# Turning one batch's q and k by the DMA crossbar and rearranging the loads around the turns, in an attention + MLP kernel

## The chip, the cores and the metric

One core of one Trainium2 chip. The metric is device time of one execution in microseconds (us), lower is better. Most executions of one kernel agree within 1.5%. TensorE is called PE, VectorE DVE, ScalarE ACT, GpSimd POOL, SyncE SP. SP computes nothing here: it only issues DMAs, one after the other. The granted clock of a view is the share of its full clock rate at which PE was allowed to run.

## The reference, cut to what matters

```python
def _attn_ref(q, k, v, lam):                 # q, k, v: (4, 8, 768, 64) float32
    for b in range(nb):                      # blocks of 64 positions
        intra = einsum('bhic,bhjc->bhij', qb, kb) * Dmask[None]
        intra = einsum('bhij,bhjd->bhid', intra, vb)
        inter = einsum('bhid,bhde->bhie', qb * lam_pow[None], kv_state)
        out[:, :, sl] = intra + inter
        kv_state = lam_block * kv_state + einsum('bhsd,bhse->bhde', kb * rev_pow, vb)

def reference(...):
    x = attention output as (3072 tokens, 512)
    h = x @ w_in                             # 512 -> 2048
    g = h * (1.0 / (1.0 + exp(-1.702 * h)))
    return g @ w_out                         # 2048 -> 512
```

## The kernel before

The kernel goes through six waves of 512 tokens. For each wave it computes attention, then MLP1 (w_in), then MLP2 (w_out). Attention of wave w+1 runs between the MLP matmuls of wave w. Waves 0 and 1 have two half waves, each of 256 positions of one batch ("batch 0" and "batch 1" of wave 1 below: `c` = 0 and 1). Waves 2 to 5 take 128 positions of all four batches.

Scores need q and k with the head dimension on the partitions, so both must be transposed ("turned"). PE can do it (`turn_pe`, 8 matmuls against an identity, then a copy out of PSUM), or the DMA crossbar (`turn_dma`):

```python
    def turn_dma(w, c, nm):
        y = work.tile([P, 2 * NP, P], bf16, tag=f"{nm}T{c}", name=f"{nm}T")
        nc.sync.dma_start_transpose(out=y, in_=cast[w, c, nm].rearrange("p b c -> p (b c)"))
        trans[w, c, nm] = y
```

Before, waves 0 and 1 are turned by PE, waves 2 to 5 by the crossbar. `do_cast` is the DVE instruction that makes `ks` and `qs` (bf16) out of the loaded k and q; a turn waits for it. Loads, crossbar turns and output stores all go through SP, in program order. The order of everything beside the MLP is set by positions among the MLP items:

```python
        for w in range(NW):
            n = len(main)
            main += mlp_items(w)
            e = len(main)
            x = w + 1
            if x < ND:                                  # ND = 2: attention of wave 1
                for c in range(HF):
                    t, d = n + 24 + 5 * c, n + 19 + 7.5 * c
                    side += [(d, (do_cast, x, c, "k", nc.vector)), ...
                             (t, (turn_pe, x, c, "k", (act_copy, dve_copy)[c])),
                             (t + 1 + c, (turn_pe, x, c, "q", (act_copy, dve_copy)[c])),
                             (t + 3, (start, x, c)), (t + 6 - c, (end, x, c))]
            elif x < NW:
                for c in range(HF):
                    tk, tq = (n + 2.1 + 2 * c, n + 4 + c) if x == ND else (n + 4 + 2 * c, n + 5 + 2 * c)
                    side += [(tk, (do_cast, x, c, "k", nc.vector)), (tk, (turn_dma, x, c, "k")),
                             (tq, (do_cast, x, c, "q", nc.vector)), (tq, (turn_dma, x, c, "q")), ...]
                if x == ND:
                    side += [(n + 7, (stores,))]        # wave 0's eight output stores, kept back till here
                t = n + 16
                side += [(t, (n_two, x, 0)), (t + 4, (n_two, x, 1)), (t + 9, (n_rest, x))]
            if w + 2 < NW:
                side += [(n + (12 if w else 20), (load, w + 2))]
```

`n_two` are the scores of a wave. PE runs them in order: the first four matmuls need the turned k and q of the first two batches (c = 0), the next four those of the other two (c = 1), and so on in turn. So the last q turn holds up all but the first four of a group of 16.

Of the kernel before, what the change touches and what calls it, by code (L numbers as in the profile page):

```python
# [24 lines left out]
def kernel(  # L25
# [13 lines left out]
    nc = tc.nc  # L39
    f32 = mybir.dt.float32  # L40
    bf16 = mybir.dt.bfloat16
    B, H, S, D = q.shape
# [3 lines left out]
    ND = 2  # L46
# [14 lines left out]
    NW = S // P  # L61
# [9 lines left out]
    HF = 2  # L71
# [64 lines left out]
    def fill(n, new=False):  # L136
        if new:
            fill_ps[0] = ps.tile([P, W], f32, tag="mm", bufs=3, name="ps_fill")
        for _ in range(n):
            nc.tensor.matmul(fill_ps[0], zero[:, 0:P], zero, start=True, stop=True)  # L140
# [47 lines left out]
    cast, trans, masked, xT, g_of, h_ps, o_ps, t_ps = {}, {}, {}, {}, {}, {}, {}, {}  # L188

    def acc(name, dt=f32, shape=None, tag="a"):  # L190
        return ps.tile(shape or [P, 4, P], dt, tag=tag, bufs={"a": 5, "mm": 3}[tag], name=name)
# [35 lines left out]
    def turn_pe(w, c, nm, copy=act_copy, g=None):  # L227
        x = cast[w, c, nm]
        rr = list(range(NP)) if g is None else [2 * g, 2 * g + 1]
        t = acc("ps_t", bf16, [P, len(rr), 2, P])  # L230
        for i, r in enumerate(rr):
            for a in range(2):
                nc.tensor.transpose(t[:, i, a, :], x[:, a, r * P : (r + 1) * P], ident)
        if g in (None, 0):
            trans[w, c, nm] = work.tile([P, 2 * NP, P], bf16, tag=f"{nm}T{c}", name=f"{nm}T")
        copy(trans[w, c, nm][:, 2 * rr[0] : 2 * rr[0] + 2 * len(rr)], t.rearrange("p r a s -> p (r a) s"))

    def turn_dma(w, c, nm):
        y = work.tile([P, 2 * NP, P], bf16, tag=f"{nm}T{c}", name=f"{nm}T")
        nc.sync.dma_start_transpose(out=y, in_=cast[w, c, nm].rearrange("p b c -> p (b c)"))  # L240
        trans[w, c, nm] = y

    def q_of(w, c, rows, r, blk):
        return trans[w, c, "q"][rows, 2 * r : 2 * r + 2, D * blk : D * blk + D]

    def d_scores(w, c, pp):
        kT = trans[w, c, "k"]
        s2 = [acc("ps_s") for _ in range(2)]
        for i in range(2):
            r = 2 * pp + i  # L250
            for a in range(2):
                for blk, bs in enumerate((A, Z)):
                    for h, hs in enumerate((A, Z)):
                        nc.tensor.matmul(s2[h][bs, 2 * i + a, :], kT[hs, 2 * r + a, bs], q_of(w, c, hs, r, blk),  # L254
                                         start=True, stop=True)
        for h in range(2):
            sm = work.tile([P, 2, 2, P], bf16, tag="sm", bufs=8, name="sm")
            nc.vector.tensor_tensor(sm.rearrange("p i a s -> p i (a s)"), s2[h].rearrange("p (i a) s -> p i (a s)", i=2),  # L258
                                    mask_d.rearrange("p o a b s -> p o (a b s)").to_broadcast([P, 2, 2 * P]), op=MUL)
            masked[w, c, pp, h] = sm  # L260
# [145 lines left out]

    def mlp_items(w):
        if w < ND:
            f = 4 if w == 0 else 8
            items = [(mlp1_half, w, c, fc) for c in range(HF) for fc in range(0, f, 2) if w or c or fc]  # L410
            items += [(mlp1, w, fc) for fc in range(f, FFC)]
        else:
            items = [(mlp1, w, fc) for fc in range(FFC)]
        if w == 0:
            items += [(mlp2, w, g, j) for j in range(NCH) for g in range(3)]
            return items + [(mlp2, w, 3, j) for j in range(NCH)]
        items += [(mlp2, w, g, j) for g in range(G) for j in range(NCH)]
        if w == NW - 1:
            items = items[:-NCH]
            for c0, c1 in ((0, 256), (256, 384), (384, 512)):  # L420
                items += [(mlp2, w, G - 1, j, c0, c1) for j in range(NCH)]
        return items

    def gate_pool(x):
        nc.gpsimd.tensor_copy(behind_q, x)
# [4 lines left out]
    with tc.manual_schedule():  # L430
        u32 = mybir.dt.uint32
        for x in kv_sb:
            nc.vector.memset(x.rearrange("p b r s -> p (b r s)").bitcast(u32), 0)
        nc.scalar.activation(warm, q_pow[:, 0, 0:1], GELU)
        fill(5)
        for g in range(2):
            do_cast(0, 0, "k", nc.vector, g)
            turn_pe(0, 0, "k", act_copy, g)
            fill(2)
        for g in range(2):  # L440
            do_cast(0, 0, "q", nc.vector, g)
            turn_pe(0, 0, "q", act_copy, g)
            fill(2 - 2 * g)
        gate_pool(loaded[0, 0, "v"][0:1, 0, 0:1])
        load_w_in(0)
        cast_v(0, 0, (act_copy, act_copy))
        d_scores(0, 0, 0)
        fill(1)
        d_scores(0, 0, 1)
        fill(3)  # L450
        for g in range(2):
            do_cast(0, 1, "k", nc.gpsimd, g)
        for j in (1, 2):
            load_w_in(j)
        one = d_state(0, 0, False, "mm")
        two = d_state(0, 0, True, "mm")
        fill(1)
        d_keep(*one)
        d_keep(*two)
        oa, oz = d_out(0, 0, "mm")  # L460
        d_x(0, 0, 0, oa, act_copy)
        d_x(0, 0, 1, oz, act_copy)
        do_cast(0, 1, "q", nc.vector, 0)
        do_cast(0, 1, "q", nc.vector, 1)
        turn_pe(0, 1, "k", dve_copy)
        turn_pe(0, 1, "q", act_copy, 0)
        fill(2, True)
        turn_pe(0, 1, "q", act_copy, 1)
        fill(2)
        cast_v(0, 1, (act_copy, pool_copy))  # L470
        for j in range(3, len(IN_CH)):
            load_w_in(j)
        for j in range(NCH):
            load_w_out(j)
        nc.gpsimd.affine_select(mask, mask, pattern=[[0, 1], [1, P]], channel_multiplier=-1, base=0,
                                compare_op=mybir.AluOpType.is_ge, fill=0.0)
        gate_sync(w_out_sb[1][0:1, 0, 0:2])
        load(1)
        d_scores(0, 1, 0)
        mlp1_half(0, 0, 0)  # L480
        d_scores(0, 1, 1)
        fill(1)
        one = d_state(0, 1, False)
        two = d_state(0, 1, True)
        d_keep(*one)

        def finish(w, c, two=None):
            oa, oz = d_out(w, c)
            d_x(w, c, 0, oa, act_copy)
            d_x(w, c, 1, oz, dve_copy)  # L490
            if two:
                d_keep(*two)

        def start(w, c):
            for pp in range(2):
                d_scores(w, c, pp)
            d_keep(*d_state(w, c, False))

        def end(w, c):
            finish(w, c, d_state(w, c, True))  # L500

        def stores():
            for f in late:
                f()

        side, main = [(0, (finish, 0, 1, two))], []
# [3 lines that stand above are left out]
            e = len(main)  # L510
            x = w + 1
            if x < ND:
                for c in range(HF):
                    t, d = n + 24 + 5 * c, n + 19 + 7.5 * c
                    side += [(d, (do_cast, x, c, "k", nc.vector)), (d + 1 + 0.5 * c, (do_cast, x, c, "q", nc.vector)),
                             (d, (cast_v, x, c)),
                             (t, (turn_pe, x, c, "k", (act_copy, dve_copy)[c])),
                             (t + 1 + c, (turn_pe, x, c, "q", (act_copy, dve_copy)[c])),
                             (t + 3, (start, x, c)), (t + 6 - c, (end, x, c))]
            elif x < NW:  # L520
                for c in range(HF):
                    tk, tq = (n + 2.1 + 2 * c, n + 4 + c) if x == ND else (n + 4 + 2 * c, n + 5 + 2 * c)
                    side += [(tk, (do_cast, x, c, "k", nc.vector)), (tk, (turn_dma, x, c, "k")),
                             (tq, (do_cast, x, c, "q", nc.vector)), (tq, (turn_dma, x, c, "q")),
                             (n + 6 + 2 * c, (cast_v, x, c))]
                if x == ND:
                    side += [(n + 7, (stores,))]
                t = n + 16
                side += [(t, (n_two, x, 0)), (t + 4, (n_two, x, 1)), (t + 9, (n_rest, x))]
            if w + 2 < NW:  # L530
                side += [(n + (12 if w else 20), (load, w + 2))]
        side.sort(key=lambda x: x[0])
        for i, (f, *a) in enumerate(main):
            while side and side[0][0] <= i:
                _, (g, *b) = side.pop(0)
                g(*b)
            f(*a)
# [30 lines left out]
```

## Time and profile before

| | before |
|---|---|
| time, median of its 4 runs at the comparison | 211.81 us (210.77 to 213.98) |
| profiled execution, span | 208.6 us |
| PE busy | 203.5 us (98%) |
| wave 2's last q turn issued / PE starts wave 2's scores | 61.96 / 66.23 us |
| granted PE clock | full in all slices |

First, the page of the kernel before, parts 1 and 2: busy time per engine; then the busy share in tenths in 40 slices of the span.

```profile
PE 203.5 (98%) x1835; PEld 107.3 (51%) x1835; DVE 94.6 (45%) x134; ACT 85.1 (41%) x156; POOL 23.8 (11%) x41
...
PE   7999999999999999999999999999999999999994
...
PEclk9999999999999999999999999999999999999999
DMA  5999999999998999998996599990480011100112
```

PE has no gap after the start. Through nearly the whole first half of the span the DMA engines too are at 90% or more. The second view is the timeline of SP, 38 to 70 us (start, length of the issue, what it issues, how many):

```profile
40.51 5.34 SPq L85 DMA_DIRECT2D kf<-in_k_dram  x2
45.94 4.60 SPq L85 DMA_DIRECT2D qf<-in_q_dram  x2
50.63 4.81 SPq L85 DMA_DIRECT2D vf<-in_v_dram  x2
55.55 3.40 SPq L240 DMA_TRANSPOSE kT<-ks  x1
59.06 1.23 SPq L240 DMA_TRANSPOSE qT<-qs  x1
60.40 1.46 SPq L240 DMA_TRANSPOSE kT<-ks  x1
61.96 2.13 SPq L240 DMA_TRANSPOSE qT<-qs  x1
64.14 5.07 SPq L400 DMA_DIRECT2D out_dram<-o_sb  x8
```

These are wave 2's six loads, wave 2's four turns, then the eight stores. A load alone is issued in 0.4 to 0.6 us, here each takes about 2.4 us. The queue seems to be full, so that an issue goes in as an earlier transfer comes out: the issues end at 45.9, 48.3 and 50.5 us, and by the trace's semaphore records earlier loads land at 46.1, 48.1 and 50.9. By the same records wave 2's last q turn landed at 66.0 us. PE's timeline shows when it is needed:

```profile
66.23 0.62 PE L305 MATMUL ps_s<-qT,kT 64*128 64x128 bf16 x16
66.78 3.63 PE L390 MATMUL ps_out<-w_out,g_sb 128*128 128x512 bf16 x16
```

The turn arrives 0.3 us before PE uses it.

### The profile page before, as it was taken

The numbers are of one execution on the slowest core, as the hardware profiler recorded it, in microseconds if no ns is written. First come the engines' busy times: TensorE is split into PE (matmuls) and PEld (weight loads), VectorE is DVE, ScalarE is ACT, GpSimd is POOL, SyncE is SP. The second block draws the span as 40 slices with busy tenths as digits, with TensorE's granted clock in tenths as the row PEclk, the third lists the DMA queues.
The fourth block names the chain that finished last, engine by engine and source line by source line (L and its number), as shares of the span: only waits on it lengthen the run. The fifth ranks groups of instructions, "written<-read, shape, count | busy, mean of one in ns | idle before, by whom it ended". The sixth has DMA issues, their size and how long they took to land.

```text
span 208.6 us, 4297 instructions
## 1 busy us (share of the span) xinstructions
PE 203.5 (98%) x1835; PEld 107.3 (51%) x1835; DVE 94.6 (45%) x134; ACT 85.1 (41%) x156; POOL 23.8 (11%) x41
## 2 busy tenths in 40 slices
PE   7999999999999999999999999999999999999994
PEld 2567444557864464444464444464444464444453
DVE  5674000689932837841747811748821731100121
ACT  5986661224765030566030466030466030566000
POOL 4377000110050000400003000030000000000000
PEclk9999999999999999999999999999999999999999
DMA  5999999999998999998996599990480011100112
GB/s 160 302 240 208 203 207 270 288 249 229 215 188 172 214 221 208 229 172 184 219 218 165 147 178 228 222 235 0 143 162 0 34 72 50 50 0 3 50 50 101
DMA packets 87640, 33.82 MB, mean 162 GB/s; under 512 B 67398, under 2 KB 84678, under 8 KB 87622
## 3 DMA queue, kind: packets, MB, share of 16 engines
q1 hardware_dynamic: 82868, 29.37, 66.4%
q0 software_dynamic: 4752, 4.19, 12.5%
q8 instruction: 14, 0.23, 0.5%
q14 instruction: 4, 0.03, 0.0%
q10 hardware_dynamic: 2, 0.00, 0.0%
HBM read 27.26 MB, written 6.29 MB: 161 GB/s over the span
## 4 chain that ended last, share of the span: by engine, by line
PE 88%; DMA 6%; DVE 3%; SPq 1%; issue 1%; POOL 0%; DVEq 0%
PE ps_out L390 39%; PE ps_h L366 35%; PE ps_h L378 5%; DMA w_in<-in_moe_w_in_dram 3%; DMA vf<-in_v_dram 2%; PE ps_s L305 2%; PE ps_o L351 2%; PE ps_o L354 2%; DVE sm L258 1%; SPq L81 1%; PE ps_kv L329 1%; PE ps_kv L269 1%; PE ps_o L284 1%; DVE ks L200 1%; DVE qs L200 1%
## 5 line engine op out<-in xcount | busy, mean ns | idle before, releaser
L390 PE MATMUL ps_out<-w_out,g_sb 128*128 128x512 bf16 (+2 forms) x416 | 86.2, 363 | 0.0
L366 PE MATMUL ps_h<-xT,w_in 128*128 128x512 bf16 x336 | 73.5, 379 | 0.0
L368 ACT ACTIVATE g_sb<-ps_h 128x512 bf16<-128x512 f32 x84 | 50.1, 597 | 47.8 <-PE ps_h L366 47.8
L390 PEld LDWEIGHTS <-g_sb 128*128 128x128 bf16 x416 | 38.2, 98 | 41.0
L366 PEld LDWEIGHTS <-w_in 128*128 128x128 bf16 x336 | 32.8, 98 | 39.2
L394 DVE COPY o_sb<-ps_out 128x512 f32<-128x512 f32 (+2 forms) x26 | 16.9, 650 | 45.4 <-PE ps_out L390 45.3
L312 DVE SCALAR_TENSOR_TENSOR sm<-ps_s,inv_pow,mask 128x512 bf16<-128x512 f32 x32 | 21.8, 743 | 32.4 <-PE ps_s L305 24.7
L210 POOL CAST v_sb<-vf 128x1024 bf16<-128x1024 f32 (+1 forms) x13 | 12.1, 942 | 111.1 <-DMA vf<-in_v_dram 87.5
L358 ACT CAST xT<-ps_o 128x512 bf16<-128x512 f32 x16 | 8.2, 600 | 36.5 <-PE ps_o L354 36.5
L334 DVE SCALAR_TENSOR_TENSOR kv<-kv,blk_pow,ps_kv 64x256 bf16<-64x256 bf16 x24 | 11.5, 480 | 7.8 <-PE ps_kv L329 4.7
L200 DVE TENSOR_TENSOR ks<-kf,kd_pow 128x512 bf16<-128x512 f32 (+1 forms) x4 | 3.7, 954 | 19.1 <-DMA kf<-in_k_dram 17.8
L378 PE MATMUL ps_h<-xT,w_in 128*128 128x256 bf16 x96 | 11.4, 273 | 0.4 <-DMA w_in<-in_moe_w_in_dram 0.4
L258 DVE TENSOR_TENSOR sm<-ps_s,mask_d 128x512 bf16<-128x512 f32 x16 | 10.0, 684 | 3.5 <-PE ps_s L254 3.5
L140 PE MATMUL ps_fill<-zero 128*128 128x512 bf16 x25 | 9.3, 477 | 1.4 <-DVE zero L113 1.4
L205 DVE TENSOR_TENSOR ks<-kf,k_pow 128x1024 bf16<-128x1024 f32 x8 | 10.5, 1317 | 0.1
L205 DVE TENSOR_TENSOR qs<-qf,q_pow 128x1024 bf16<-128x1024 f32 x8 | 10.6, 1322 | 0.0
L378 PEld LDWEIGHTS <-w_in 128*128 128x128 bf16 x96 | 8.9, 98 | 2.0 <-DMA w_in<-in_moe_w_in_dram 0.5
L380 ACT ACTIVATE g_sb<-ps_h 128x512 bf16<-128x512 f32 x12 | 7.2, 597 | 5.0 <-PE ps_h L378 4.8
L351 PEld LDWEIGHTS <-kv 128*64 128x64 bf16 x128 | 7.0, 110 | 1.7 <-issue 1.7
L351 PE MATMUL ps_o<-qT,kv 128*64 128x128 bf16 x128 | 7.7, 221 | 0.0
L354 PE MATMUL ps_o<-sm,v_sb 128*64 128x128 bf16 x128 | 7.6, 219 | 0.0
L275 ACT CAST kv<-ps_kv 64x256 bf16<-64x256 f32 x16 | 5.9, 366 | 3.2 <-PE ps_kv L269 3.0
(59 smaller groups left out, 90.9 us busy)
## 6 DMA issues: line engine op xcount, KB each, us to landing
vf<-in_v_dram SPq DMA_DIRECT2D x11, 512.0 KB, 7.4
kf<-in_k_dram SPq DMA_DIRECT2D x10, 512.0 KB, 6.1
qf<-in_q_dram SPq DMA_DIRECT2D x10, 512.0 KB, 7.4
out_dram<-o_sb SPq DMA_DIRECT2D x15, 256.0 KB, 2.0
out_dram<-o_sb SPq DMA_DIRECT2D x17, 128.0 KB, 2.4
w_out<-in_moe_w_out_dram POOLq DMA_DIRECT2D x4, 512.0 KB, 14.0
w_in<-in_moe_w_in_dram POOLq DMA_DIRECT2D x3, 512.0 KB, 7.9
kf<-in_k_dram SPq DMA_DIRECT2D x4, 256.0 KB, 3.4
```

The source lines that it names most:

```text
L205: eng.tensor_tensor(x.rearrange("p b (h d) -> p b h d", h=H), f.rearrange("p (b h) (a d) -> p b (h a) d", b=2, a=2), pw.unsqueeze(3).to_br ...
L210: nc.gpsimd.tensor_copy(out, in_)
L258: nc.vector.tensor_tensor(sm.rearrange("p i a s -> p i (a s)"), s2[h].rearrange("p (i a) s -> p i (a s)", i=2), mask_d.rearrange("p o a b ...
L312: nc.vector.scalar_tensor_tensor(sm, s, inv_pow[:, 2 * p + h : 2 * p + h + 1], mask.to_broadcast([P, B, P]), op0=MUL, op1=MUL)
L334: nc.vector.scalar_tensor_tensor(new[hs, :, p, hs], old[hs, :, p, hs], blk_pow[hs, 2 * p + h : 2 * p + h + 1], ps_kv[hs, i], op0=MUL, op1=ADD)
L351: nc.tensor.matmul(ps_o[hs, b, :], kv[:, b, p, hs], qT[:, (b % 2) * NP + p, :], start=(b == 0), stop=False, skip_group_check=True)
L354: nc.tensor.matmul(ps_o[hs, b, :], vt[:, b, 2 * p + h, :], masked[w, p, h][:, b, :], start=False, stop=True, skip_group_check=True)
L366: nc.tensor.matmul(h, w_in_sb[j][:, kc, i * P : (i + 1) * P], xT[w][:, kc, :], start=(kc == 0), stop=(kc == KC - 1))
L368: nc.scalar.activation(g_of[w][:, fc, :], h, GELU)
L378: nc.tensor.matmul(h[:, u, :], w_in_sb[j][:, kc, i * P : (i + 1) * P], xT[w][:, kc, cols], start=(kc == 0), stop=(kc == KC - 1))
L390: nc.tensor.matmul(ps_out, g_of[w][:, fc, g * P : (g + 1) * P], w_out_sb[j][:, fc % CW, c0:c1], start=(fc == 0), stop=(fc == FFC - 1))
L394: nc.vector.tensor_copy(o, ps_out)
```

## The change

Intent: take 16 transposes and two PSUM copies of batch 1 of wave 1 away from PE and DVE and give them to the crossbar; run wave 1's MLP1 all in half waves, so that batch 1's attention has more time; place wave 2's loads around the new turns, which go through the same queue; compute wave 2's scores two MLP items later. The diff, cut to its core (`turned` only gives the other layout that the crossbar writes):

```diff
-            f = 4 if w == 0 else 8
+            f = 4 if w == 0 else 16
...
-                for c in range(HF):
-                    t, d = n + 24 + 5 * c, n + 19 + 7.5 * c
-                    side += [ ... casts, turn_pe of both batches, start, end ... ]
+                t = n + 24
+                side += [(n + 19, (do_cast, x, 0, "k", nc.vector)), (n + 20, (do_cast, x, 0, "q", nc.vector)),
+                         (n + 19, (cast_v, x, 0)), (t, (turn_pe, x, 0, "k")), (t + 1, (turn_pe, x, 0, "q")),
+                         (t + 2.5, (do_cast, x, 1, "k", nc.vector)), (t + 2.5, (turn_dma, x, 1, "k")),
+                         (t + 2.5, (load_one, 2, 0, "k", k)), (t + 3, (start, x, 0)),
+                         (t + 3.5, (do_cast, x, 1, "q", nc.vector)), (t + 3.5, (turn_dma, x, 1, "q")),
+                         (t + 3.5, (load_one, 2, 1, "k", k)), (t + 3.5, (load, 2, "qv")), (t + 3.5, (cast_v, x, 1)),
+                         (t + 6, (end, x, 0)), (e + 3, (start, x, 1)), (e + 6, (end, x, 1))]
...
-                    tk, tq = (n + 2.1 + 2 * c, n + 4 + c) if x == ND else (n + 4 + 2 * c, n + 5 + 2 * c)
+                    tk, tq = (n + 2.9 + 3.2 * c, n + 6.1 + c) if x == ND else (n + 4 + 2 * c, n + 5 + 2 * c)
...
                 if x == ND:
                     side += [(n + 7, (stores,))]
-                t = n + 16
+                t = n + (18 if x == ND else 16)
...
-            if w + 2 < NW:
-                side += [(n + (12 if w else 20), (load, w + 2))]
+            if 0 < w < NW - 2:
+                side += [(n + 12, (load, w + 2))]
```

More of the change, by code (lines that the diff above doesn't have):

```diff
@@ L241, in turn_dma, with turned @@
         trans[w, c, nm] = y
+    def turned(w, c, nm):
+        return trans[w, c, nm].rearrange("p (r a) s -> p r a s" if (w, c) != (1, 1) else "p (a r) s -> p r a s", a=2)
     def q_of(w, c, rows, r, blk):
-        return trans[w, c, "q"][rows, 2 * r : 2 * r + 2, D * blk : D * blk + D]
+        return turned(w, c, "q")[rows, r, :, D * blk : D * blk + D]
     def d_scores(w, c, pp):
-        kT = trans[w, c, "k"]
+        kT = turned(w, c, "k")
         s2 = [acc("ps_s") for _ in range(2)]
@@ L253, in d_scores @@
                     for h, hs in enumerate((A, Z)):
-                        nc.tensor.matmul(s2[h][bs, 2 * i + a, :], kT[hs, 2 * r + a, bs], q_of(w, c, hs, r, blk),
+                        nc.tensor.matmul(s2[h][bs, 2 * i + a, :], kT[hs, r, a, bs], q_of(w, c, hs, r, blk),
                                          start=True, stop=True)
@@ L512 @@
             if x < ND:
-                for c in range(HF):
-                    t, d = n + 24 + 5 * c, n + 19 + 7.5 * c
-                    side += [(d, (do_cast, x, c, "k", nc.vector)), (d + 1 + 0.5 * c, (do_cast, x, c, "q", nc.vector)),
-                             (d, (cast_v, x, c)),
-                             (t, (turn_pe, x, c, "k", (act_copy, dve_copy)[c])),
-                             (t + 1 + c, (turn_pe, x, c, "q", (act_copy, dve_copy)[c])),
-                             (t + 3, (start, x, c)), (t + 6 - c, (end, x, c))]
+                t = n + 24
[6 more added lines that the diff above has]
+                         (t + 6, (end, x, 0)), (e + 3, (start, x, 1)), (e + 6, (end, x, 1))]
             elif x < NW:
                 for c in range(HF):
-                    tk, tq = (n + 2.1 + 2 * c, n + 4 + c) if x == ND else (n + 4 + 2 * c, n + 5 + 2 * c)
+                    tk, tq = (n + 2.9 + 3.2 * c, n + 6.1 + c) if x == ND else (n + 4 + 2 * c, n + 5 + 2 * c)
                     side += [(tk, (do_cast, x, c, "k", nc.vector)), (tk, (turn_dma, x, c, "k")),
```

## The prediction

> **What bounds the kernel now.** TensorE. The page gives PE 203.5 of 208.6 us busy; the chain of waits is 88% PE. Matmuls follow each other without a gap: in the chain 64 of 512 columns take 13.81 us (216 ns each), 40 of 256 columns 4.47 us (112 ns each). Only the stretch from 43 to 51 us hangs on VectorE (ks, sm, qs, kT, xT, o_sb, qT); PE waits there add up to about 0.6 us.
>
> **What the change takes away.** 16 PE transposes (8 in 0.45 us, twice: 0.9 us of PE), two VectorE copies of 0.69 us and most of that 0.6 us. MLP1 in half waves swaps 32 matmuls of 216 ns for 64 of 112 ns: +0.2 us. Alone that is worth about 1 us, 0.5%.
>
> **What it adds.** Two DMA transposes and a new order on the one SyncE queue, where an issue blocks. Wave 2's loads land about 2.4 us apart (48 to 60 us): limited by the transfer. Before, these six are issued from 40.5 to 55.4 us; wave 2's four turns from 55.55 to 64.1, the last landing at about 66.0, just ahead of the scores at 66.3. Then eight stores, 0.63 us of issue each, 5.1 us together.
>
> After, by the compiled order: turn k, load k0, turn q, load k1, q0, q1, v0, v1, turns k, q, k, then the eight stores, only then wave 2's last q turn. Batch 1's q turn waits for VectorE's qs (47.23 + 1.2 us), so it is issued at about 48.5 and lands at about 52 (3.3 us), when PE wants it (51.8): a wait of 0 to 1 us. Five loads follow from 49.8: 4.8 us for the first (as at 69.25), 2.4 for each other, so the last lands at about 64 instead of 60. Three turns go out behind it until about 65.3, the stores until 70.4, the last q turn lands at about 73.5. Wave 2's scores, now two MLP2 groups later, could start at 67.2. PE works in order, so it should stall about 6 us in the first score group. The equivalent point before is 68.0: +5.5 us net on the critical path.
>
> **Clock.** "TensorE: Matmul & The Clock Gate" in the Trainium skill, Part 1, says that the array falls to half clock after an idle window of about 3.4 us, until busy for about as long. The trace agrees on the cold rate: the first 512-column matmuls start every 427 ns, from 6.8 us on every 216 ns. A stall of 6 us should cost another 1 to 2 us (estimate from that page). From wave 3 on everything is as before, only later.
>
> **Sum.** 212.8 + 5.5 to 6.5 (the saving is in it) + 0 to 2, shaded for doubt: about 218.8 us, range 212.5 to 222.5. Faster by over 2%: 0.03; within 2%: 0.31; slower by over 2%: 0.66.
>
> **What would show it.** Timeline: PE idle for 4 to 7 us inside wave 2's first scores (L308), ended by the DMA of qT; 512-column matmuls at about 430 ns for some us after. SyncE: wave 2's last load issued until about 59 us, stores from about 65, last q turn at about 70. No transposes (L233) after 42 us; L381 x160. A PE gap under 1 us before batch 1's scores (L257, about 52 us).
>
> **What would make it wrong.** The queue may move faster: if the turns don't wait behind the v loads (3.4 us for the first now), or loads land closer than 2.4 us, the stall falls to 3 us or less and the result is within 2%. The timings look tuned, and on the chip a stall of 6 us would have been seen; so I leave 0.31 to "same". If the clock does not fall, about 218.

## The result, and the profile after

222.06 us median (221.74 to 222.72, 4 runs) against 211.81 before. The ratio is 1.0505, 95% interval 1.043 to 1.058: slower. Ratios here and below are the mean time of one kernel's fast runs over the mean of the kernel before's fast runs of the same rounds, so they are not quite the ratio of the medians. The medians are over all runs, with one slow one in each of three sets: the kernel before here (213.98), experiment 1 (218.74) and the last run of experiment 7 (214.38).

The page of the changed kernel, parts 1 and 2:

```profile
PE 203.3 (92%) x1826; PEld 110.5 (50%) x1851; DVE 92.1 (42%) x132; ACT 85.4 (39%) x156; POOL 23.0 (10%) x41
...
PE   7979999998996099999999999999999999999994
...
PEclk9999999999999559999999999999999999999999
DMA  5999999979998999949999459999194011200112
```

PE's busy time is the same, 203.3 us (the part at half clock included); the span grew by 11.3 to 219.9. (The profiled execution of the kernel before took 210.6 us in all, less than each of its four runs; so the two spans differ by more than the medians.) In slice 14 (counted from one) PE is idle, and in slices 14 and 15 the granted clock is half. SP's timeline, 46 to 77 us:

```profile
46.29 1.79 SPq L240 DMA_TRANSPOSE kT<-ks  x1
48.13 0.58 SPq L85 DMA_DIRECT2D kf<-in_k_dram  x1
49.81 1.92 SPq L240 DMA_TRANSPOSE qT<-qs  x1
51.83 0.53 SPq L85 DMA_DIRECT2D kf<-in_k_dram  x1
52.41 4.08 SPq L85 DMA_DIRECT2D qf<-in_q_dram  x2
56.59 5.13 SPq L85 DMA_DIRECT2D vf<-in_v_dram  x2
61.81 3.48 SPq L240 DMA_TRANSPOSE kT<-ks  x1
65.40 2.01 SPq L240 DMA_TRANSPOSE qT<-qs  x1
67.51 1.28 SPq L240 DMA_TRANSPOSE kT<-ks  x1
68.84 5.10 SPq L403 DMA_DIRECT2D out_dram<-o_sb  x8
74.06 1.29 SPq L240 DMA_TRANSPOSE qT<-qs  x1
```

Wave 2's last q turn is issued at 74.06 and not at 61.96 us. Of these 12.1 us the stores in front of it are 5.1, the rest is that everything before it is later. PE's timeline shows what that does:

```profile
67.43 1.89 PE L393 MATMUL ps_out<-w_out,g_sb 128*128 128x512 bf16 x7
69.63 0.29 PE L308 MATMUL ps_s<-qT,kT 64*128 64x128 bf16 x4 [0.31 <-DMA qT<-qs]
77.30 0.82 PE L308 MATMUL ps_s<-qT,kT 64*128 64x128 bf16 x12 [7.39 <-DMA qT<-qs]
78.06 5.59 PE L393 MATMUL ps_out<-w_out,g_sb 128*128 128x512 bf16 x16
```

The bracket gives the idle time in front of a group and what ended it. After four score matmuls PE waits 7.39 us for the DMA of qT. Then the same 16 matmuls of MLP2 that took 3.63 us take 5.59. The windows view (stretch, busy time by engine, granted clock, DMA share, GB/s) gives the clock, and also a hole in the DMA at 46 to 52 us:

```profile
46.00:52.00 6.00, 5.80 (x83) 3.54 (x83) 5.08 (x8) 1.69 (x5) 1.18 (x2) 1.00 0.76 152
69.90:77.30 7.40, 0.02 (x1) 0.09 (x1) 0.00 (x0) 0.00 (x0) 0.00 (x0) 0.63 0.89 190
77.30:84.00 6.70, 6.70 (x44) 2.96 (x43) 3.42 (x5) 0.00 (x0) 0.00 (x0) 0.64 1.28 231
```

The same view of the kernel before:

```profile
46.00:52.00 6.00, 5.86 (x134) 4.03 (x132) 5.49 (x10) 1.99 (x5) 1.17 (x2) 1.00 1.07 217
66.30:70.70 4.40, 4.40 (x46) 2.22 (x48) 2.98 (x5) 0.60 (x1) 0.00 (x0) 1.00 0.89 199
```

The work that takes 6.7 us at a granted clock of 0.64 took 4.4 us at 1.00: 2.3 us. The sum for the two profiles: the waits at the scores 7.39 + 0.31 = 7.7, low clock 2.3, and 1.35 us that the profiled execution was already late before batch 1 begins (after batch 0's scores PE resumes MLP2 at 43.80 us before, at 45.15 after; the program is the same up to there, the w_in and w_out loads were slower in this execution; over all the profiles taken, with the same start, PE's first turn of wave 1 lies at 39.4 to 40.4 us, but for one at 44.6). That is 11.35 of 11.3 us, so almost nothing is left for the saving that was the aim. Between that point and the end of wave 1's MLP1 the changed kernel takes 67.43 - 45.15 = 22.28 us, the one before 66.23 - 43.80 = 22.43.

### The profile page after: what moved, and what is told of

Its sections match the earlier page's. It is cut to its first block, busy times and chain, and to the rows that moved or that the text cites. A ratio compares the mean times of both kernels' runs of the same rounds, so it can differ in the third digit from the quotient of the medians.

```text
span 219.9 us, 4302 instructions
## 1 busy us (share of the span) xinstructions
PE 203.3 (92%) x1826; PEld 110.5 (50%) x1851; DVE 92.1 (42%) x132; ACT 85.4 (39%) x156; POOL 23.0 (10%) x41
## 3 DMA queue, kind: packets, MB, share of 16 engines
q0 software_dynamic: 4752, 4.19, 12.1%
## 4 chain that ended last, share of the span: by engine, by line
PE 72%; DMA 16%; SPq 6%; DVE 2%; issue 1%; POOL 1%
PE ps_out L393 33%; PE ps_h L369 25%; DMA w_out<-in_moe_w_out_dram 7%; PE ps_h L381 5%; DMA qf<-in_q_dram 3%; SPq L81 3%; DMA qT<-qs 3%; DMA vf<-in_v_dram 3%; SPq L403 2%; PE ps_s L308 2%; PE ps_o L354 2%; PE ps_o L357 2%; DVE o_sb L397 1%; PE ps_kv L332 1%; POOL w_in L178 1%
## 5 line engine op out<-in xcount | busy, mean ns | idle before, releaser
L369 PE MATMUL ps_h<-xT,w_in 128*128 128x512 bf16 x299 | 66.2, 379 | 0.3
L369 PEld LDWEIGHTS <-w_in 128*128 128x128 bf16 x304 | 29.8, 98 | 35.6
L210 POOL CAST v_sb<-vf 128x1024 bf16<-128x1024 f32 (+1 forms) x13 | 11.3, 877 | 123.9 <-DMA vf<-in_v_dram 72.9
L381 PE MATMUL ps_h<-xT,w_in 128*128 128x256 bf16 x160 | 18.3, 273 | 0.8 <-DMA w_in<-in_moe_w_in_dram 0.8
L381 PEld LDWEIGHTS <-w_in 128*128 128x128 bf16 x160 | 15.2, 98 | 3.4 <-DMA w_in<-in_moe_w_in_dram 0.9
L308 PE MATMUL ps_s<-qT,kT 64*128 64x128 bf16 x128 | 5.5, 226 | 7.7 <-DMA qT<-qs 7.7
L205 DVE TENSOR_TENSOR ks<-kf,k_pow 128x1024 bf16<-128x1024 f32 x8 | 9.8, 1221 | 2.0 <-ACT g_sb L383 1.9
L205 DVE TENSOR_TENSOR qs<-qf,q_pow 128x1024 bf16<-128x1024 f32 x8 | 9.8, 1219 | 0.4 <-DMA qf<-in_q_dram 0.4
L140 PE MATMUL ps_fill<-zero 128*128 128x512 bf16 x22 | 8.5, 500 | 1.4 <-DVE zero L113 1.4
L308 PEld LDWEIGHTS <-kT 64*128 64x128 bf16 x128 | 4.0, 98 | 11.2 <-issue 10.1
```

The source lines that it names most:

```text
L205: eng.tensor_tensor(x.rearrange("p b (h d) -> p b h d", h=H), f.rearrange("p (b h) (a d) -> p b (h a) d", b=2, a=2), pw.unsqueeze(3).to_br ...
L210: nc.gpsimd.tensor_copy(out, in_)
L308: nc.tensor.matmul(s2[h][:, b, :], kT[hs, (b % 2) * NP + p, :], qT[hs, (b % 2) * NP + p, :], start=True, stop=True)
L369: nc.tensor.matmul(h, w_in_sb[j][:, kc, i * P : (i + 1) * P], xT[w][:, kc, :], start=(kc == 0), stop=(kc == KC - 1))
L381: nc.tensor.matmul(h[:, u, :], w_in_sb[j][:, kc, i * P : (i + 1) * P], xT[w][:, kc, cols], start=(kc == 0), stop=(kc == KC - 1))
```

## The experiments

First theory, A: the eight stores in front of the last q turn make the stall. Rivals: B, wave 2's loads are late and the stores sit in their shadow; C, crossbar turns or half waves cost by themselves.

### 1. Stores behind the last turn

```diff
-                    side += [(n + 7, (stores,))]
+                    side += [(n + 7.2, (stores,))]
```

> The changed kernel, with one move: wave 2's last q turn is issued ahead of the eight stores of wave 0 and not behind them. Theory A (the stores' 5.1 us of issue in front of that turn make most of the PE stall of 7.7 us): the turn is issued at about 69 us, lands at about 72, PE's wait in wave 2's first scores falls to 2 to 3 us, the clock is not lowered or only briefly, time about 214.5 to 217 us. Rival B (the stall comes from wave 2's loads being late, and the stores only sit in the shadow): stall still over 5 us, time over 219. Rival C (crossbar turns are slow in themselves, queue order does not matter): as B.

Measured: 215.61 us, ratio 1.0169 (1.007 to 1.027). PE's timeline:

```profile
71.00 0.51 PE L308 MATMUL ps_s<-qT,kT 64*128 64x128 bf16 x12 [2.47 <-DMA qT<-qs]
```

The wait falls from 7.7 to 2.47 us, by about the stores' 5.1. A holds for the larger part, 3.4 of 5.05%. But 2.5 us of lateness stay, and in the profiled run the clock still falls after so short a wait (in another run, 215.14 us, the mean granted clock is 0.999).

### 2. The v loads behind the turns too

```diff
-                         ... (t + 3.5, (load, 2, "qv")), ...
+                         ... (t + 3.5, (load, 2, "q")), ...
-                             (n + 6 + 2 * c, (cast_v, x, c))]
+                             (n + (7.3 if x == ND else 6) + 2 * c, (cast_v, x, c))]
-                    side += [(n + 7, (stores,))]
+                    side += [(n + 7.15, (load, 2, "v")), (n + 7.2, (stores,))]
```

> The changed kernel with wave 2's v loads and the stores both moved behind wave 2's four turns; batch 1 of wave 1 still turned by the crossbar, MLP1 still in half waves. Theory A (all of the loss is the place in the SyncE queue): the last q turn lands at about 66 us, no stall in wave 2's first scores, no low clock, time about 211 to 212.5, the same as before. Rival C (crossbar turns of batch 1 or the half waves cost by themselves): stays over 215.

Measured: 218.37 us, ratio 1.030 (1.021 to 1.039). Neither expectation was right: wave 2 has no wait any more (its 16 matmuls run in one piece from 69.05 us), and yet the kernel is slower than in experiment 1. The wait has moved to wave 3:

```profile
101.23 0.31 PE L308 MATMUL ps_s<-qT,kT 64*128 64x128 bf16 x4 [2.38 <-DMA qT<-qs]
104.33 0.82 PE L308 MATMUL ps_s<-qT,kT 64*128 64x128 bf16 x12 [2.79 <-DMA qT<-qs]
```

SP's timeline of the same run shows what stands in front of wave 3's turns, the last of which is issued at 100.96:

```profile
88.27 7.91 SPq L403 DMA_DIRECT2D out_dram<-o_sb  x8
96.34 1.31 SPq L240 DMA_TRANSPOSE kT<-ks  x1
```

Theory A was too small. The reading is that the queue as a whole is late, and what is late is carried along until PE needs it. The new theory, D: from wave 1 to wave 3 the queue is as tight as PE, and any time that it lies idle or is given more to do comes out as a wait at the next score group.

### 3. The kernel before with only the stores moved ahead of the last turn

```diff
-                    side += [(n + 7, (stores,))]
+                    side += [(n + 4.5, (stores,))]
```

> The kernel before with one move: the eight stores issued ahead of wave 2's last q turn. No other part of the change. Theory A: the turn that was issued at 61.95 and landed at 66 now lands at about 71; PE wanted it at 66.3, so it stalls about 4.5 to 5 us, long enough for the low clock: time about 6 to 7 us longer, 218 us. Rival B or C (order of stores is harmless): within 1 us of before.

Measured: 218.35 us, ratio 1.030 (1.021 to 1.039). The profiled execution started 5 us late for another reason (see the last section) and PE waited 2.90 us.

> One more profile of the kernel before with the stores ahead of the last q turn: the first one fell in an execution whose start was 5 us late for another reason (first w_in load at 17.5 and not 15.1 us, clock low until 25.7 us), which hides part of the stall. With a normal start I expect the last q turn to land at 70 to 71 us, a stall of 4 to 5 us in wave 2's first scores, the clock low for 3 to 7 us after, and a total of 217 to 218 us. If the start is late again, that is part of this kernel and not chance.

217.22 us in one run (state unknown, as for any single run), with a normal start. PE's timeline:

```profile
71.51 0.82 PE L305 MATMUL ps_s<-qT,kT 64*128 64x128 bf16 x12 [4.93 <-DMA qT<-qs]
```

One position in the queue, without any other part of the change, costs a wait of 4.93 us and 3% of the time. This kernel has no late loads and no added crossbar turns, so rivals B and C do not explain that.

### 4. Batch 1 turned by PE, all else as changed

```diff
-                         ... (t + 2.5, (turn_dma, x, 1, "k")),
+                         ... (t + 5, (turn_pe, x, 1, "k", dve_copy)),
-                         ... (t + 3.5, (turn_dma, x, 1, "q")),
+                         ... (t + 7, (turn_pe, x, 1, "q", dve_copy)),
```

> The changed kernel with one part undone: batch 1 of wave 1 turned by PE as before; the order of loads, stores and wave 2's turns as changed, half waves as changed. Nothing in the SyncE queue then holds wave 2's loads back. If the stores' place makes most of the loss whatever turns batch 1: the last q turn still lands at 70 to 71 us, PE wants it at about 68, stall 2 to 4 us and the low clock, 215 to 217 us. If the crossbar turns are needed for the loss: 211 to 212.

Measured: 215.88 us, ratio 1.020 (1.014 to 1.025). The loads are issued early again (v until 55.9 us), the stores still stand ahead of the last q turn, issued at 68.12, and PE waits 3.05 us:

```profile
71.38 0.82 PE L308 MATMUL ps_s<-qT,kT 64*128 64x128 bf16 x12 [3.05 <-DMA qT<-qs]
```

So a loss of 2% needs no added crossbar turn; experiment 3 shows that the stores' place is enough for one of this size. Taking the turns out took 3.1 of the 5.05% away, taking the stores out of the way (experiment 1) 3.4. The two shares overlap and are not to be added: a wait is what is left of both delays after the slack, and the clock can fall with either. It need not: in two of the four runs here the mean granted clock is 1.000, in the others 0.982 and 0.990.

### 5. Half waves alone

The kernel before with `f = 16` for wave 1.

> The kernel before with wave 1's MLP1 all in half waves and nothing else. All theories that put the loss in the queue: 0.2 us longer by matmul pace (64 of 112 ns for 32 of 216), within 0.5 us of before. If the half waves cost in themselves (weight loads not hidden behind 256 columns): 1 us or more longer.

Measured: 211.43 us, ratio 0.999 (0.995 to 1.004). The half waves are innocent.

### 6. The loads held back, nothing else

The kernel before, with wave 2's loads behind a 4-byte copy that waits for batch 1's ks.

```diff
+            if w == 0:
+                side += [(n + 27, (gate_k,)), (n + 27, (load, w + 2))]
```

> The kernel before with none of the change: only wave 2's six loads are held back in the SyncE queue until batch 1's ks is written (by a 4-byte copy out of ks issued ahead of them), as the crossbar turn of k does in the changed kernel. PE keeps its transposes, MLP1 keeps full waves, stores stay behind the last turn. New theory D (in waves 1 to 3 the SyncE queue is as tight as PE: the last q turn of waves 2 and 3 lands only 0.3 us before PE wants it, so any time that the queue lies idle comes out as a PE stall): loads start at about 46 and not 40.5 us, the last q turn of wave 2 lands at about 70 to 71, PE stalls 4 to 5 us, plus the low clock: 216 to 218 us. Rival A (what costs is the stores' place alone): within 1 us of before.

Measured: 213.12 us, ratio 1.006 (1.0015 to 1.011). PE waits 1.24 us in wave 2's scores, where it did not wait before, and the clock stays up:

```profile
68.55 0.51 PE L305 MATMUL ps_s<-qT,kT 64*128 64x128 bf16 x12 [1.24 <-DMA qT<-qs]
```

D is right in kind and wrong by a factor of 3 to 4 in size. The issue started 5.9 us later than before, but the last load of wave 1 was still moving: by the semaphore records it landed at 46.9 us, and wave 2's first load at 51.7, where at the usual pace of 2.4 us it could have landed at 49.3. About 2.4 us of transfer time were lost, not 5.9 (the last q turn landed at 68.5 us, 2.5 later than before); and this execution had its own late start, so that PE came 0.8 us later too.

### 7. Refill the queue, and then make room in wave 3

Experiment 7a is experiment 2 with both k loads of wave 2 issued ahead of batch 1's turns, batch 1's scores one item later, and two of wave 2's turns (the first q, the second k) one item later. Experiment 7b is 7a with one more move, wave 1's eight stores behind wave 3's turns:

```diff
 7a
+                         (t + 2.5, (load_one, 2, 0, "k", k)), (t + 2.5, (load_one, 2, 1, "k", k)),
+                         (t + 2.5, (do_cast, x, 1, "k", nc.vector)), (t + 2.5, (turn_dma, x, 1, "k")), ...
+                         ... (e + 4, (start, x, 1)), (e + 7, (end, x, 1))]
+                    tk, tq = (n + 2.9 + 4.2 * c, n + 7.1 + 0.01 * c) if x == ND else ...
 7b, on top
-                late.append(store) if w == 0 else store()
+                late.append(store)                     # and the list is emptied when it is flushed
+                if x == ND + 1:
+                    side += [(n + 7.2, (stores,))]
```

> The changed kernel with the queue refilled: both k loads of wave 2 issued ahead of batch 1's turns (so that the DMA has work while the turns wait for VectorE), v loads and stores of wave 0 behind wave 2's turns, batch 1's scores one half item later. Theory D: no stall at wave 2's scores; but the two extra turns are about 2.4 us more for the queue, so at wave 3 the last q turn comes 2 to 3 us too late: 213 to 215 us. Rival A (only the place of the stores and v loads counts): as the second run, 218. Rival E (wave 3's stall in that run was chance): 211.

> The run above, with wave 1's eight stores (5.1 us of issue) also moved, behind wave 3's turns. Theory D: the queue gets 5 us of slack where wave 3 needs it, no stall over 1 us anywhere, time 210 to 211.5: at or a little below the kernel before. If it stays at 213 or more, D lacks something.

Measured: 7a 217.84 us, ratio 1.027 (1.021 to 1.033); 7b 211.09 us, ratio 0.997 (0.9915 to 1.002). 7a waits 1.72 + 2.67 us in wave 3's scores and then runs at the low clock:

```profile
100.80 0.29 PE L308 MATMUL ps_s<-qT,kT 64*128 64x128 bf16 x4 [1.72 <-DMA qT<-qs]
103.76 0.82 PE L308 MATMUL ps_s<-qT,kT 64*128 64x128 bf16 x12 [2.67 <-DMA qT<-qs]
```

(I had expected 2 to 3 us and 213 to 215 us; the direction is D's, the size again not.) In 7b SP issues wave 3's turns first, from 86.75 us on, and then the stores:

```profile
94.05 1.27 SPq L240 DMA_TRANSPOSE qT<-qs  x1
95.37 5.07 SPq L403 DMA_DIRECT2D out_dram<-o_sb  x8
```

and PE does not wait in wave 2's or wave 3's scores. Its timeline there has the 16 matmuls of each group in one piece, without a bracket; the line of wave 3:

```profile
97.30 0.62 PE L308 MATMUL ps_s<-qT,kT 64*128 64x128 bf16 x16
```

The pair 7a and 7b differs in nothing but the place of eight stores, and that is 3% of the time. 7b holds the crossbar turns and the half waves, so with room in the queue they cost nothing that the times show. (The kernel before with its stores placed as in 7b was not run. Its PE is busy for 98% of the span and waits nowhere for the queue, so there is little that late stores could gain there and hide here.) It was run once more in five rounds:

> The same kernel as the run with wave 1's stores behind wave 3's turns, in five rounds, to see whether it is under the kernel before and not only equal. By PE work: 0.9 us less transposes, 0.2 us more half waves, 0.6 us of VectorE waits gone or replaced: 0.5 to 1 us faster, ratio 0.995 to 0.998. If the queue order only hides a cost: ratio 1.000 or more.

Measured: 211.53 us, ratio 0.9975 (0.992 to 1.003). It is within the expected range, but the interval contains 1: that it beats the kernel before is not shown.

### 8. What the low clock costs

The changed kernel, with matmuls of zeros in the stall to keep PE busy.

```diff
+        def keep_busy():
+            fill(32, True)          # 44 in the second try
...
+                    side += [(n + 7, (stores,)), (n + 17.9, (keep_busy,))]
```

> The changed kernel with 32 matmuls of zeros (216 ns each, 6.9 us) put into the stall, just ahead of wave 2's first scores. They keep PE busy while it waits and change nothing that it waits for. If the low clock after the stall costs what I read (about 2.2 us: 16 matmuls in 5.5 us where 3.5 would do), the granted clock stays at full speed in all slices and the time falls by about 2 us against the changed kernel, to about 220. If the clock record is only a by-product and costs nothing, the time is the same 222 (or longer, if the fill overshoots the wait).

With 32: 221.76 us, ratio 1.0455 (1.035 to 1.056), inconclusive: in this execution the turn came so late that 2.68 us of waiting were left after the fill, and the clock fell after all. So a second try:

> The changed kernel with 44 matmuls of zeros in the stall instead of the 32 of the earlier run, whose fill ended 2.7 us before the turn landed and so let the clock fall after all (3.4 us at half). 44 x 0.216 = 9.5 us reach to about the landing. If the low clock costs time: no slice below full clock after the stall, wave 2's first 28 score matmuls with the MLP2 groups between take 4.4 us as before and not 6.7, and the time is about 2 us under the changed kernel: 220, ratio 1.035 to 1.042. If it does not: ratio 1.05.

With 44: 220.75 us, ratio 1.043 (1.036 to 1.050), against 1.0505 for the changed kernel. The page has full clock in all 40 slices, and the windows view gives the stretch after the fill:

```profile
78.50:83.00 4.50, 4.50 (x48) 2.32 (x48) 3.32 (x5) 0.00 (x0) 0.00 (x0) 1.00 1.20 234
```

The work after the stall takes 4.5 us again and not 6.7. By the ratios that is 0.7%, 1.5 us; the intervals of the two ratios overlap, so the size rests on the windows (2.2 us less) more than on the times. The two profiles differ by 1.0 us only (218.9 and 219.9): with the fill the turn landed at 78.4 us, in the changed kernel at 77.3. Work that computes nothing made the kernel no slower, and within the profile shorter after the stall.

## Why the prediction was right or wrong

**Right: where and by what.** A PE stall inside wave 2's first scores, after the first four matmuls, ended by the DMA of qT; the stores' 5.1 us ahead of the last q turn; the fall of the clock; a wait under 1 us before batch 1's scores (0.62 us); no further transposes on PE, and 160 half-wave matmuls. "From wave 3 on everything is as before" holds too: in the changed kernel PE waits for a turn in no later score group.

**Wrong: the size.** The step that failed is "**Sum.** 212.8 + 5.5 to 6.5 (the saving is in it) + 0 to 2, shaded for doubt: about 218.8". That is 6 us of loss, and the runs show 222.06 - 211.81 = 10.25 (212.8 is the median of the three runs known before). The mechanism was right; the terms were mis-sized: the stall (about 6 us, measured 7.7), the low clock (0 to 2, measured 2.3) and the saving (about 1, measured 0.15). The range reached up to 222.5, but no sum of the terms did. Four things in it:

- "PE works in order, so it should stall about 6 us": 7.7 us measured. The chain of the queue was right in order but short: I let wave 2's first three turns go out "until about 65.3"; they went out until 68.8. Of these 3.5 us, 1.3 were there when batch 1's q turn was issued (49.81 us and not 48.5; as much as this execution was late on PE). The other 2.2 were added in thirds by issues that took longer than I had put in: that turn (1.92 us), the five loads behind it (until 61.7 and not 59), and wave 2's turns (the second took 2.01 us, where 1.23 is usual). PE was late too, ready at 69.3 us and not at 67.2, which is why only 1.7 us more of waiting came of it.
- "about 1 us" of saving: 0.15 us measured between the two fixed points. The transposes' 0.9 us went into the wait of 0.62 for batch 1's q turn and the 0.2 of the half waves, and batch 0's outputs now wait for the masks (32 matmuls in 0.91 us, 0.64 before).
- "another 1 to 2 us", entered in the sum as "0 to 2": 2.3 us by the windows. (How much it is depends on where the stall falls; see the last section.)
- "shaded for doubt". The terms as written reach from 218.3 to 221.3; I pulled the centre to the lower end because the timings looked tuned. The looks of a schedule are no measurement. The order of the compiled queue was, and it showed the stores ahead of the turn.

**Missed: the general reason.** I treated it as one late transfer. Experiments 2 and 7a are what a queue without slack for two waves would give: curing wave 2 alone moves the wait to wave 3 (5.2 and 4.4 us there), and only room in both (7b) brings the time back. The page "DMA: Bandwidth & Descriptors" of the Trainium skill says (section "Anatomy of one DMA — SWDGE (gpsimd) path") that DMA engines do not wait on semaphores, and that a wait happens on the issuing sequencer before dispatch. The trace agrees: behind the turn of k, which waits for DVE, wave 2's first load is issued at 48.13 us, where it was 40.51. It is only a part of the loss, though: the held-back loads alone cost 0.6% (experiment 6).

**Open.** How the 2.5 us that remain in experiment 1 divide between the hole in the DMA at 46 to 52 us (share 0.76 against 1.07) and the transfers of the two added turns was not separated. No run puts the stores' place (3.0% alone, experiment 3) and the held-back loads (0.6% alone, experiment 6) together into the kernel before, so what of the 5.05% the two make together is not shown. Which moves of 7b are needed (k loads first, v loads last) was not tried one by one.

## What to carry to other kernels

Before work is moved from a busy engine to a DMA, compare the time at which the last transfer lands with the time at which it is used: a slack of 0.3 us, as here, means that the queue is a second critical path, even if no wait shows. On an in-order queue put what a compute engine will wait for ahead of what nobody waits for, such as output stores, and check the next waves too, because lateness is carried along. A stall of PE can cost more than its length, when the low clock follows it (2.3 us here).

## What the Trainium skill lacked or had wrong

- "TensorE: Matmul & The Clock Gate", Part 1, puts the fall to half clock after at least one idle window of about 3.4 us, and calls the window free-running. Here a window that was idle for a little more than half was enough. In the clock records of these traces the stretches between two changes last whole multiples of 3.41 us (3.41, 6.83, 10.24, 13.65, 64.85 and so on), which agrees with such windows, and they can be laid over the trace. In all 14 profiles, half clock followed each window (from full clock) in which PE was idle for 58% or more (11 cases), and none in which it was idle for 56% or less. (The ends of matmuls are modelled, so these shares are rough.) So the length of a gap alone does not decide. Experiment 1's gap of 2.47 us lay in one window, idle for 2.55 of 3.41 us: the next was at half clock. The wait of 2.90 us in experiment 3's first profile was split over two, idle for 1.76 and 1.14 us: the clock stayed full. These are the two windows of experiment 1 (stretch, busy time by engine with PE first, granted clock, DMA share, GB/s):

```profile
68.09:71.50 3.41, 0.86 (x18) 0.69 (x18) 0.13 (x1) 0.00 (x0) 0.00 (x0) 1.00 0.99 196
71.50:74.91 3.41, 3.41 (x10) 1.21 (x10) 2.59 (x4) 0.00 (x0) 0.00 (x0) 0.50 0.88 200
```

These are the two of experiment 3's first profile:

```profile
70.03:73.44 3.41, 1.65 (x11) 0.63 (x10) 0.00 (x0) 1.53 (x3) 0.00 (x0) 1.00 0.95 202
73.44:76.85 3.41, 2.27 (x21) 1.22 (x21) 1.90 (x3) 0.00 (x0) 0.00 (x0) 1.00 0.92 199
```

- The same page's two rates agree with the traces: half and full clock only, 427 ns and 216 ns from start to start for 512 columns.
- "DMA: Bandwidth & Descriptors", section "Issuing engines are not separate DMA queues", says that the time to initiate a DMA is usually small relative to the DMA itself. Here the issue of eight stores, 0.59 us each and 5.1 us together (each lands about 2.4 us after its issue begins), stood in front of a transfer that PE waited for. Whether issuing them from another engine helps, no run here shows.
- No page that I read gives the issue time of a DMA on a full queue. Here: a load of 512 KB is issued in 0.4 to 0.6 us on an idle queue and 2.4 us on a full one, a store of 128 KB in 0.59 us, a crossbar turn in 1.23 us, and up to 3.5 us behind two loads; a turn lands 3.1 to 3.3 us after its issue begins on a quiet queue.
- No page that I read warns that the landing of a kernel's first loads varies by execution: the first w_in load landed at 15.1 us in one execution of the kernel before and at 17.5 in experiment 3's first profile, whose program is the same up to there. PE then waited 2.23 us, the clock was at half from 18.8 to 25.7 us, and the execution was 5 us late at wave 1.
